# One level of Strassen's scheme in both feed-forward products of a float32 kernel for retention and a squared-ReLU feed-forward

## The chip, the cores and the metric

The kernel runs on one core of a Trainium2 chip. Its time is the device time of one execution in microseconds. The kernel before was run three times; the time before is the median of these.

## What is computed

```python
# q, k, v: (8, 8, 576, 64) float32; w_in (512, 2048), w_out (2048, 512) float64
scores = matmul(q, k.T) / sqrt(64)
Dmat   = where(t >= s, gamma[h] ** (t - s), 0)        # gamma = 1 - 2**(-5 - h)
x      = matmul(scores * Dmat, v)                      # retention, per batch and head
x      = x.transpose(0, 2, 1, 3).reshape(4608, 512)    # 8 * 576 tokens, d_model 512
out    = square(maximum(x @ w_in, 0)) @ w_out          # (4608, 512) float32
```

Both weights come in as float64, as their bits, and are rounded to float32 on the chip.

## The kernel before

Retention goes over 40 chunks of 128 tokens (the fifth of each batch of 576 has 64). For chunk i, `turn(i)` transposes q and k on TensorE (VectorE scales q by gamma^t, ScalarE copies k); `scores(i)` makes the masked scores `ret0` and `ret1`, one for each head of a pair, and `vs`, v scaled by gamma^-s; `retain(i)` makes the chunk's x, transposed, from `ret` and `vs` and from U, the sum of k^T v' over the chunks before it in its batch. U of a pair of heads lies on the diagonal of a 128 x 128 block `u_sb`. The main loop interleaves `retain(i-2)`, `scores(i-1)` and `turn(i)`, and after each of the three calls `ffn(tokens / 3)`.

The feed-forward part works on nine blocks of 512 tokens. Block n starts when its x, `xT[n]`, is complete. `ffn_in(n, m)` makes one of 16 tiles of 128 of d_ff: four matmuls of 512 columns into PSUM, ReLU on ScalarE into `r`, the square on VectorE into `g`. `ffn_out(n, ts, part)` sums a quarter of d_ff for 128 tokens; after the last quarter VectorE copies the sum and POOL's queue stores it. `ffn` takes such steps from a list at a rate set by the tokens. Both weights stay on chip for the whole run.

A weight piece (512 KB of float64 bits) is fetched by `fetch_w` and rounded by `round_w`: five passes on VectorE (L122, L127 to L130) with two on POOL (L123, L125) between the first and the fourth. `prepare` rounds the next piece and fetches two ahead: three pieces for each turn of the main loop at the start, then one for each feed-forward step.

Order: every engine takes its instructions in the order in which the code issues them, and waits on semaphores. A tile pool gives out `bufs` buffers in turn; who writes to one waits until the last user of it has finished. DMAs of inputs and weights are issued on SP's queue, in that order, and a wait there holds back what follows.

Of the kernel before, what the change touches and what calls it, by code (L numbers as in the profile page):

```python
# [10 lines left out]
U32 = mybir.dt.uint32  # L11
AF = mybir.ActivationFunctionType
# [4 lines left out]
N_LD = 4  # chunks of q, k and v on chip at once  # L17
# [3 lines left out]
def kernel(  # L21
# [23 lines left out]
    nc = tc.nc  # L45
# [3 lines left out]
    HP = H // 2  # pairs of heads: a pair fills the 128 partitions  # L49
# [4 lines left out]
    N_DF = d_ff // 128  # L54
    N_BLK = n_tok // TOK
# [17 lines left out]
    ps_f = ctx.enter_context(tc.tile_pool(name="ps_f", bufs=2, space=PS))  # L73
# [23 lines left out]
    raws = []

    def fetch_w(j):
        t, src = w_tile(j)  # L100
        w.append(t)
        if src.dtype == F32:
            nc.sync.dma_start(t, src)
            raws.append(None)
            return
        raw = raw_pool.tile([128, N_DM, 128], src.dtype, tag="raw", name="raw")
        nc.sync.dma_start(raw, src)
        raws.append(raw)

    def round_w(j):  # L110
        """float64 bits to the nearest float32: (mantissa) * 2^(exponent), and the sign.
# [3 lines left out]
        if raws[j] is None:  # L115
            return
# [239 lines left out]
```

## Time and profile before

| | us |
|---|---|
| median of 3 runs | 1265.71 (1264.05 to 1266.25) |
| span of the profiled execution | 1263.9 |
| TensorE busy | 1222.0 |
| VectorE busy | 313.0 |
| ScalarE busy | 154.4 |
| GpSimd (POOL) busy | 74.9 |

The profiled execution's own time is not given apart from the runs; its span is the time from its first to its last instruction. PE is TensorE's matmul side, PEld its weight loads, DVE VectorE, ACT ScalarE, SPq and POOLq the queues that issue DMAs. L numbers are lines of the kernel. In the trace a float32 matmul of the code is two MATMUL instructions, each with a weight load of its own, and a transpose is one.

### The profile page before, as it was taken

How to read it: one execution, taken by the hardware profiler on the slowest of the kernel's cores; microseconds unless marked ns; L12 is line 12 of the kernel's file. 1: busy time of each engine (PE TensorE's matmuls, PEld its weight loads, DVE VectorE, ACT ScalarE, POOL GpSimd, SP SyncE). 2: the span in 40 equal slices, each digit the busy share in tenths (PEclk: the TensorE clock that was granted, in tenths of full speed). 3: DMA queues.
4: the chain of work that ended last, by engine and by line, in shares of the span. 5: the costliest groups of instructions: out<-in, count | busy, mean ns of one | idle time of the engine just before them, and what ended most of it. 6: DMA issues, size and time to landing. Idle time of an engine off the chain costs nothing.

```text
span 1263.9 us, 10515 instructions
## 1 busy us (share of the span) xinstructions
PE 1222.0 (97%) x4416; PEld 609.8 (48%) x4416; DVE 313.0 (25%) x500; ACT 154.4 (12%) x293; POOL 74.9 (6%) x110
## 2 busy tenths in 40 slices
PE   3698999999999999999999999999999999999998
PEld 2454544544445554445544554454544544444443
DVE  4888811221122112221112112211221122101200
ACT  1111100210012001110121001100210012000100
POOL 2333300000000000000000000000000000000000
PEclk9698999999999999999999999999999999999999
DMA  9655412001210112001110111101121000000000
GB/s 237 180 142 154 117 42 59 5 17 42 59 30 17 33 30 46 21 25 34 42 34 13 34 42 26 42 21 33 25 50 30 26 9 1 9 17 8 1 9 25
DMA packets 126479, 56.41 MB, mean 45 GB/s; under 512 B 113760, under 2 KB 121952, under 8 KB 126304
## 3 DMA queue, kind: packets, MB, share of 16 engines
q1 hardware_dynamic: 123552, 46.30, 15.9%
q0 software_dynamic: 2880, 9.44, 1.9%
q8 instruction: 35, 0.57, 0.2%
q14 instruction: 12, 0.10, 0.0%
HBM read 46.29 MB, written 9.44 MB: 44 GB/s over the span
## 4 chain that ended last, share of the span: by engine, by line
issue 72%; PE 18%; POOL 4%; DVE 4%; SPq 1%; DMA 0%; POOLq 0%
PE o_ps L262 8%; PE h_ps L248 7%; POOL exp L125 1%; POOL out_dram L268 1%; SPq L82 1%; POOL exp L123 1%; PE x_ps L215 1%; DVE w_in L129 1%; DVE w_in L130 1%; PE x_ps L212 1%; PE sc L193 1%; PE u_ps L231 1%; DVE exp L122 1%; DMA raw<-in_moe_w_in_dram 0%; DVE ret L198 0%
## 5 line engine op out<-in xcount | busy, mean ns | idle before, releaser
L248 PE MATMUL h_ps<-xT,w_in 128*128 128x512 f32 x1152 | 509.4, 596 | 0.0
L262 PE MATMUL o_ps<-w_out,g 128*128 128x512 f32 x1152 | 506.7, 594 | 0.0
L248 PEld LDWEIGHTS h_ps<-xT,w_in 128*128 128x128 f32 x1152 | 215.3, 191 | 253.0 <-issue 250.5
L262 PEld LDWEIGHTS o_ps<-w_out,g 128*128 128x128 f32 x1152 | 214.8, 190 | 253.5 <-issue 249.7
L253 DVE TENSOR_TENSOR g<-r 128x512 f32<-128x512 f32 x144 | 99.5, 691 | 405.6 <-ACT r L251 405.6
L251 ACT ACTIVATE r<-h_ps 128x512 f32<-128x512 f32 x144 | 86.0, 597 | 512.4 <-PE h_ps L248 487.5
L198 DVE TENSOR_TENSOR ret<-sc,msk 128x512 f32<-128x512 f32 (+1 forms) x80 | 47.0, 629 | 213.8 <-PE sc L193 213.8
L268 POOL DMA_DIRECT2D out_dram<-o_sb x36 | 19.6, 545 | 1084.0 <-DVE o_sb L266 1084.0
L266 DVE COPY o_sb<-o_ps 128x512 f32<-128x512 f32 x36 | 24.9, 692 | 202.1 <-PE o_ps L262 202.1
L215 PE MATMUL x_ps<-ret,vs 128*64 128x128 f32 (+1 forms) x640 | 65.0, 296 | 0.2 <-DVE vs L202 0.2
L212 PE MATMUL x_ps<-qT,u_sb 128*128 128x128 f32 (+1 forms) x256 | 60.3, 319 | 0.2 <-DVE ret L198 0.2
L212 PEld LDWEIGHTS x_ps<-qT,u_sb 128*128 128x128 f32 x256 | 42.4, 197 | 29.4 <-issue 27.8
L183 ACT COPY kT<-kT_ps 128x512 f32<-128x512 f32 (+1 forms) x40 | 21.7, 543 | 282.7 <-PE kT_ps L178 282.4
L193 PEld LDWEIGHTS sc<-qT,kT 64*128 64x128 f32 (+1 forms) x640 | 37.1, 183 | 32.1 <-issue 30.9
L225 ACT COPY xT<-x_ps 128x512 f32<-128x512 f32 (+1 forms) x44 | 22.0, 509 | 235.2 <-PE x_ps L215 235.2
L178 PE MATMUL kT_ps<-ident,k_ld 128*128 128x128 f32 (+1 forms) x160 | 25.1, 283 | 26.5 <-DVE ret L198 26.4
L181 DVE TENSOR_TENSOR qT<-qT_ps,dq 128x512 f32<-128x512 f32 (+1 forms) x40 | 25.3, 633 | 100.5 <-PE qT_ps L178 90.5
L193 PE MATMUL sc<-qT,kT 64*128 64x128 f32 (+1 forms) x640 | 44.5, 280 | 5.2 <-DVE qT L181 5.2
L215 PEld LDWEIGHTS x_ps<-ret,vs 128*64 128x64 f32 (+1 forms) x640 | 33.8, 141 | 20.7 <-issue 6.9
L231 PE MATMUL u_ps<-vs,k_ld 128*128 128x128 f32 x256 | 39.2, 299 | 0.0
L231 PEld LDWEIGHTS u_ps<-vs,k_ld 128*128 128x128 f32 x256 | 33.0, 201 | 6.0 <-issue 6.0
L178 PEld LDWEIGHTS kT_ps<-ident,k_ld 128*128 128x128 f32 (+1 forms) x160 | 18.8, 149 | 28.2 <-DVE ret L198 27.7
(25 smaller groups left out, 253.3 us busy)
## 6 DMA issues: line engine op xcount, KB each, us to landing
out_dram<-o_sb POOLq DMA_DIRECT2D x36, 256.0 KB, 2.3
q_ld<-in_q_dram SPq DMA_DIRECT2D x32, 256.0 KB, 4.5
k_ld<-in_k_dram SPq DMA_DIRECT2D x32, 256.0 KB, 3.3
v_ld<-in_v_dram SPq DMA_DIRECT2D x32, 256.0 KB, 4.1
raw<-in_moe_w_in_dram SPq DMA_DIRECT2D x16, 512.0 KB, 4.4
raw<-in_moe_w_out_dram SPq DMA_DIRECT2D x16, 512.0 KB, 3.4
dq<-in_decay_q_dram SPq DMA_DIRECT2D x1, 1152.0 KB, 7.1
q_ld<-in_q_dram SPq DMA_DIRECT2D x8, 128.0 KB, 2.9
```

What stands on the lines that cost most here:

```text
L178: nc.tensor.transpose(p[:, hp, :cs], loaded[i][j][:cs, 2 * hp:2 * hp + 2, :], ident[:cs, :cs])
L181: nc.vector.tensor_tensor(t[:, :, :cs], p[:, :, :cs], dq[:, :, c0:c0 + cs], op=ALU.mult)
L193: nc.tensor.matmul(sc[e][:cs, hp, :cs], lhsT=kT[sl, hp, :cs], rhs=qT[sl, hp, :cs], start=True, stop=True)
L198: nc.vector.tensor_tensor(r[:cs, :, :cs], sc[e][:cs, :, :cs], msk[:cs, :, :cs].to_broadcast([cs, HP, cs]), op=ALU.mult)
L212: nc.tensor.matmul(p[:, hp, :cs], lhsT=u_sb[ci % 2][:, hp, :], rhs=s["qT"][:, hp, :cs], start=True, stop=False, skip_group_check=True)
L215: nc.tensor.matmul(p[D * e:D * e + D, hp, :cs], lhsT=s["vs"][:cs, 2 * hp + e, :], rhs=s["ret"][e][:cs, hp, :cs], start=(ci == 0), stop=Tru ...
L231: nc.tensor.matmul(u_ps[0][:, hp, :], lhsT=loaded[i][1][:cs, 2 * hp:2 * hp + 2, :], rhs=s["vs"][:cs, 2 * hp:2 * hp + 2, :], start=(ci == 0 ...
L248: nc.tensor.matmul(p, lhsT=w[m][:, cc, :], rhs=xT[n][:, cc, :], start=(cc == 0), stop=(cc == N_DM - 1))
L251: nc.scalar.activation(r, p, AF.Relu)
L253: nc.vector.tensor_tensor(g[n, m], r, r, op=ALU.mult)
L262: nc.tensor.matmul(acc[0], lhsT=g[n, m][:, ts * 128:(ts + 1) * 128], rhs=w[N_DF + m].rearrange("p c f -> p (c f)"), start=(m == 0), stop=( ...
L268: nc.gpsimd.dma_start(out[row:row + 128, :], o)
```

## The change

The first block is still computed plainly, but its second product runs with d_ff outside: `first_out(m)` adds two tiles of d_ff to four sums in PSUM. Beside it POOL makes Strassen's sums of the weights: those of w_in in place and in `ws` (`sum_w_in`), those of w_out in a `stage` tile that then goes, with all seven operands, to DRAM (`w2_dram`). There are two `stage` tiles, and a pair of pieces of w_out is rounded straight into one.

From block 1 on both products are taken as 2 x 2 blocks in seven half-size products (`PRODUCTS`; each right operand is 256 columns wide). `sum_x` makes the sums of x, partly in place. `ffn_in(n, mp, j)` does product j for two pairs of d_ff tiles, and adds what comes out of PSUM to earlier parts on VectorE and ScalarE; POOL makes the sums of the squared values for the second product. `ffn_out(n, j, tt)` takes its right operand from `w2`, 1 MB for each product, which `fetch_w2` brings from DRAM for step j+2 when step j is done.

In retention, U and its part of x are made in tiles of 64 columns (of the lhsT), so that only the diagonal of U is computed; `vs` moves from VectorE to POOL; `kT`, `ret` and `vs` have one buffer instead of two, q and v three instead of four. Fetched float64 bits and exponents lie in parts of `G` (g2 and g3) that are not yet in use. `ps_f` has four PSUM buffers of one kind instead of two of each of two kinds.

```diff
+PRODUCTS = (
+    ("A11", "B11", "a"), ("S2", "T2", "b"), ("S1", "T1", "c"), ("A12", "B21", "a"),
+    ("S3", "T3", "b"), ("S4", "B22", "c"), ("A22", "T4", "b"),
+)
+OPENS = {0, 1, 2}
+CLOSES = {3, 5, 6}
...
-    ps_f = ctx.enter_context(tc.tile_pool(name="ps_f", bufs=2, space=PS))
+    ps_f = ctx.enter_context(tc.tile_pool(name="ps_f", bufs=4, space=PS))
+    wa = [const.tile([128, N_DM, 128], F32, name=f"wa{m}") for m in range(N_M)]
+    wb = [const.tile([128, N_DM, 128], F32, name=f"wb{m}") for m in range(N_M)]
+    ws = [const.tile([128, 3, 2, 128], F32, name=f"ws{m}") for m in range(N_M)]
+    G = [const.tile([128, 7, 2, HT], F32, name=f"g{j}") for j in range(N_M // 2)]
+    w2_dram = dram.tile([7, 128, N_M, d_model // 2], F32, name="w2_dram")
...
+    def piece_dst(j):
+        wi, m, e = pieces[j]
+        if wi == 0:
+            return (wb if e else wa)[m].rearrange("p c f -> p (c f)")
+        if e == 0:
+            stage[m] = w2_pool.tile([128, N_M, d_model // 2], F32, tag="w2", name="w2_stage")
+        return stage[m][:, 2 * e:2 * e + 2, :].rearrange("p a b -> p (a b)")
...
     def retain(i):
...
             if ci > 0:
-                nc.tensor.matmul(p[:, hp, :cs], lhsT=u_sb[ci % 2][:, hp, :], rhs=s["qT"][:, hp, :cs], ...)
+                for e in range(2):
+                    half = slice(D * e, D * e + D)
+                    nc.tensor.matmul(p[half, hp, :cs], lhsT=u_sb[ci % 2][:, hp, half], rhs=s["qT"][:, hp, :cs], ...)
...
-                nc.tensor.matmul(u_ps[0][:, hp, :], lhsT=loaded[i][1][:cs, 2 * hp:2 * hp + 2, :],
-                                 rhs=s["vs"][:cs, 2 * hp:2 * hp + 2, :], ...)
+                for e in range(2):
+                    nc.tensor.matmul(u_ps[0][D * e:D * e + D, hp, :], lhsT=loaded[i][1][:cs, 2 * hp + e, :],
+                                     rhs=s["vs"][:cs, 2 * hp + e, :], ...)
...
+    def first_in(m):                       # m: 0 to 15, tiles m // 2 and m // 2 + 8 in turn
...
+        r = work2.tile([128, TOK], F32, tag="qT", name="r")
+        nc.scalar.activation(r, p, AF.Relu)
+        nc.vector.tensor_tensor(g0(m + e * N_M), r, r, op=ALU.mult)
+    def sum_w_in(m):
+        nc.gpsimd.tensor_tensor(s1, a21, a22, op=ALU.add)
+        nc.gpsimd.tensor_tensor(s2, s1, a11, op=ALU.subtract)
+        nc.gpsimd.tensor_tensor(s4, a12, s2, op=ALU.subtract)
+        nc.gpsimd.tensor_tensor(a21, a11, a21, op=ALU.subtract)
+    def first_out(m):
+        s = stage[m]
+        for e in range(2):
+            for ts in range(N_TS):
+                nc.tensor.matmul(acc[ts], lhsT=g0(m + e * N_M)[:, ts * 128:(ts + 1) * 128],
+                                 rhs=s[:, 2 * e:2 * e + 2, :].rearrange("p a b -> p (a b)"), ...)
+        sum_w_in(m)
+        b11, b12, b21, b22, t1, t2, t4 = (s[:, j, :] for j in range(7))
+        nc.gpsimd.tensor_tensor(t1, b12, b11, op=ALU.subtract)
+        nc.gpsimd.tensor_tensor(t2, b22, t1, op=ALU.subtract)
+        nc.gpsimd.tensor_tensor(t4, b21, t2, op=ALU.subtract)
+        nc.gpsimd.tensor_tensor(b12, b22, b12, op=ALU.subtract)
+        nc.sync.dma_start(w2_dram[:, :, m, :].rearrange("o p d -> p o d"), s[:, 0:7, :])
...
+    def sum_x(n):
+        nc.vector.tensor_tensor(t1, b12, b11, op=ALU.subtract)
+        nc.vector.tensor_tensor(t2, b22, t1, op=ALU.subtract)
+        nc.gpsimd.tensor_tensor(b12, b22, b12, op=ALU.subtract)
+        nc.gpsimd.tensor_tensor(t4, b21, t2, op=ALU.subtract)
...
+    def ffn_in(n, mp, j):
+        if mp == 0 and j == 0:
+            for nxt in range(2):
+                fetch_w2(nxt)
+        left, right, to = PRODUCTS[j]
+        if j in OPENS:
+            sums[to] = ps_f.tile([128, 2, HT], F32, tag="f", name=f"h_{to}")
+        p = sums[to]
+        for mm in range(2):
+            w = w1(left, 2 * mp + mm)
+            for c in range(2):
+                nc.tensor.matmul(p[:, mm, :], lhsT=w[:, c, :], rhs=xs[n][right][:, c, :], ...)
+        def square(t):
+            nc.vector.scalar_tensor_tensor(t, t, 0.0, t, op0=ALU.max, op1=ALU.mult)
+        if j == 0:
+            nc.scalar.copy(p1, p)
+        elif j == 1:
+            nc.vector.tensor_tensor(u2, p, p1, op=ALU.add)
+        elif j == 2:
+            nc.scalar.copy(p15, p)
+            nc.vector.tensor_tensor(p15, p15, p1, op=ALU.add)
+        elif j == 3:
+            nc.scalar.activation(g["A11"], p, AF.Relu)
+            nc.gpsimd.tensor_tensor(g["A11"], g["A11"], g["A11"], op=ALU.mult)
+        elif j == 4:
+            nc.vector.tensor_tensor(g["A22"], p, p15, op=ALU.add)
+            square(g["A22"])
+        elif j == 5:
+            nc.vector.tensor_tensor(g["S1"], p, u2, op=ALU.add)
+            square(g["S1"])
+            nc.gpsimd.tensor_tensor(g["S3"], g["A11"], g["S1"], op=ALU.subtract)
+            nc.gpsimd.tensor_tensor(g["S1"], g["S1"], g["A22"], op=ALU.add)
+            nc.gpsimd.tensor_tensor(g["S2"], g["S1"], g["A11"], op=ALU.subtract)
+        else:
+            nc.vector.tensor_tensor(g["A12"], p, p1, op=ALU.add)
+            square(g["A12"])
+            nc.gpsimd.tensor_tensor(g["S4"], g["A12"], g["S2"], op=ALU.subtract)
+    def ffn_out(n, j, tt):
...
+        for m in range(N_M):
+            nc.tensor.matmul(p[:, tt, :], lhsT=G[m // 2][:, G_SLOT[left], m % 2, tt * 128:(tt + 1) * 128],
+                             rhs=w2[j][:, m, :], ...)
+        if tt == 0:
+            return
+        if j + 2 < len(PRODUCTS):
+            fetch_w2(j + 2)
...
+    def block_steps(n):
+        if n == 0:
+            return ([(4, first_in, m) for m in range(N_DF)] + [(8, first_out, m) for m in range(N_M)])
+        return ([(2, ffn_in, n, mp, j) for mp in range(N_M // 2) for j in range(len(PRODUCTS))]
+                + [(4, ffn_out, n, j, tt) for j in range(len(PRODUCTS)) for tt in range(2)])
     def ffn(tokens):
-        owed[0] += tokens * PER_TOK
-        while steps and owed[0] >= 1:
+        owed[0] += tokens * 118 / TOK
+        while steps and owed[0] >= steps[0][0]:
+            cost, f, *args = steps.pop(0)
+            for _ in range(cost // 4 if f in (first_in, first_out) else 0):
+                prepare(min(len(pieces) - 1, 2 * N_M + 3 + (2 * args[0] if f == first_out else 0)))
```

How the instructions stand on the engines, at three places. First TensorE, around the end of the `retain` of chunk 11 (the second of the third batch), with block 1's second product on either side of it. Before (`o_ps` is a sum of the second product, `g` its left operand; a row is one matmul of the code, or several alike):

```order
L212 MATMUL x_ps_1594<-qT_1466,u_sb0_132 128x128
L215 MATMUL x_ps_1594<-ret0_1542,vs_1546 64x128
L215 MATMUL x_ps_1594<-ret1_1544,vs_1546 64x128
L231 MATMUL u_ps_1387<-vs_1546,k_ld_1212 128x128 x4
L262 MATMUL o_ps_1589<-w_out4_636,g_1289 128x512
L262 MATMUL o_ps_1589<-w_out5_677,g_1318 128x512
L262 MATMUL o_ps_1589<-w_out6_713,g_1343 128x512
L262 MATMUL o_ps_1589<-w_out7_747,g_1366 128x512
```

Now (`o_a` and `o_b` are sums of two of Strassen's products, `w2` their right operands, g0 to g3 the tiles of `G`):

```order
L258 MATMUL x_ps_1618<-qT_1449,u_sb1_148 64x128 x2
L262 MATMUL x_ps_1618<-ret0_1542,vs_1546 64x128
L262 MATMUL x_ps_1618<-ret1_1544,vs_1546 64x128
L279 MATMUL u_ps_1487<-vs_1546,k_ld_1160 64x64 x8
L431 MATMUL o_a_1609<-w2_1286,g0_116 128x256 x2
L431 MATMUL o_a_1609<-w2_1286,g1_117 128x256 x2
L431 MATMUL o_a_1609<-w2_1286,g2_118 128x256 x2
L431 MATMUL o_a_1609<-w2_1286,g3_119 128x256 x2
L431 MATMUL o_b_1659<-w2_1288,g0_116 128x256 x2
```

Columns of 512 became 256, U's parts became 64 wide and twice as many.

Second VectorE in block 0, where pieces of w_out are rounded; before, while the first product runs (`w_out4` and `w_out5` are pieces that stay on chip):

```order
L122 TENSOR_SCALAR exp_716<-raw_637 128x512 [waits DMAHW6_49]
L127 TENSOR_SCALAR w_out4_636<-raw_637 128x512
L128 SCALAR_TENSOR_TENSOR w_out4_636<-raw_637,w_out4_636 128x512 [waits DVE_49]
L129 SCALAR_TENSOR_TENSOR w_out4_636<-w_out4_636,exp_716 128x512 [waits DVE_49,Pool_49]
L130 SCALAR_TENSOR_TENSOR w_out4_636<-raw_637,w_out4_636 128x512 [waits DVE_49]
L253 TENSOR_TENSOR g_731<-r_729 128x512 [waits Activation_49]
L181 TENSOR_TENSOR qT_738<-qT_ps_733,dq_96 128x512 [waits PE_49]
```

Now, behind the scores that follow `first_out(0)` (`w2_stage_925` is the third `stage` tile, in the first one's buffer; its second write waits for a DMA and for POOL):

```order
L240 TENSOR_TENSOR ret1_920<-sc1_909,msk_144 128x512 [waits PE_49]
L165 TENSOR_SCALAR g3_119<-g2_118 128x512 [waits DMAHW6_49]
L170 TENSOR_SCALAR w2_stage_925<-g2_118 128x512 [waits DMAHW6_49,Pool_49]
L171 SCALAR_TENSOR_TENSOR w2_stage_925<-g2_118,w2_stage_925 128x512 [waits DVE_49]
L172 SCALAR_TENSOR_TENSOR w2_stage_925<-w2_stage_925,g3_119 128x512 [waits DVE_49,Pool_49]
L173 SCALAR_TENSOR_TENSOR w2_stage_925<-g2_118,w2_stage_925 128x512 [waits DVE_49]
L165 TENSOR_SCALAR g3_119<-g2_118 128x512 [waits DMAHW7_49]
L170 TENSOR_SCALAR w2_stage_925<-g2_118 128x512
```

The rounding of w_out moved from the first product, a piece a step, to the second, two pieces a step, into buffers that are used again.

Third POOL at the same place. Before, only exponents (two passes a piece) stand there:

```order
L123 TENSOR_SCALAR exp_943<-exp_943 128x512 [waits DVE_49]
L125 TENSOR_SCALAR exp_943<-exp_943 128x512 [waits Pool_49]
L123 TENSOR_SCALAR exp_963<-exp_963 128x512 [waits DVE_49]
L125 TENSOR_SCALAR exp_963<-exp_963 128x512 [waits Pool_49]
L123 TENSOR_SCALAR exp_980<-exp_980 128x512 [waits DVE_49]
```

Now (the exponents of the pair for the third `stage` tile, in g3, then the sums of `first_out(1)`; the last waits for TensorE, and SP's store of that tile waits for it):

```order
L166 TENSOR_SCALAR g3_119<-g3_119 128x512 [waits DVE_49]
L168 TENSOR_SCALAR g3_119<-g3_119 128x512 [waits Pool_49]
L166 TENSOR_SCALAR g3_119<-g3_119 128x512 [waits DVE_49]
L168 TENSOR_SCALAR g3_119<-g3_119 128x512 [waits Pool_49]
L307 TENSOR_TENSOR ws1_109<-wb1_101 128x256
L308 TENSOR_TENSOR ws1_109<-ws1_109,wa1_93 128x256 [waits Pool_49]
L309 TENSOR_TENSOR ws1_109<-wa1_93,ws1_109 128x256 [waits Pool_49]
L310 TENSOR_TENSOR wb1_101<-wa1_93,wb1_101 128x256
L328 TENSOR_TENSOR w2_stage_654<-w2_stage_654 128x256
L329 TENSOR_TENSOR w2_stage_654<-w2_stage_654 128x256 [waits Pool_49]
L330 TENSOR_TENSOR w2_stage_654<-w2_stage_654 128x256 [waits Pool_49]
L331 TENSOR_TENSOR w2_stage_654<-w2_stage_654 128x256 [waits PE_49]
```

Eight two-input passes for each `first_out` were added behind the exponents of a later pair.

More of the change, by code (lines that the diff above doesn't have):

```diff
@@ L96 @@
-    w = []
-    raws = []
-    def fetch_w(j):
[L100 to L104, printed above, removed]
-            return
[L106 to L116, printed above, removed]
-        words = raws[j].rearrange("p c f -> p (c f)").bitcast(U32).rearrange("p (n two) -> p n two", two=2)
+    pieces = [(wi, m, e) for wi in range(2) for m in range(N_M) for e in range(2)]
@@ L169 @@
     xT = {}
+    xs = {}
     u_ps = [None]
@@ new lines, in store @@
+    def store(n, half, o):
+        row = n * TOK + half * HT
+        nc.gpsimd.dma_start(out[row:row + HT, :].rearrange("(a p) d -> p a d", p=128), o)
+    def sum_x(n):
+        x = xT[n]
+        b11, b12 = x[:, 0:2, 0:HT], x[:, 0:2, HT:]
+        b21, b22 = x[:, 2:4, 0:HT], x[:, 2:4, HT:]
+        t = work.tile([128, 3, 2, HT], F32, tag="xs", name="xs")
+        t1, t2, t4 = (t[:, j, :, :] for j in range(3))
+        nc.vector.tensor_tensor(t1, b12, b11, op=ALU.subtract)
+        nc.vector.tensor_tensor(t2, b22, t1, op=ALU.subtract)
+        nc.gpsimd.tensor_tensor(b12, b22, b12, op=ALU.subtract)
+        nc.gpsimd.tensor_tensor(t4, b21, t2, op=ALU.subtract)
+        xs[n] = {"B11": b11, "T3": b12, "B21": b21, "B22": b22, "T1": t1, "T2": t2, "T4": t4}
```

204 lines of the change are left out of this document (134 added, 70 removed).

## The prediction

> **What bounds the kernel now.** I read the busy times by engine first, then who waited for whom on TensorE, then TensorE's timeline.
>
> ```profile
> span 1263.9 us, 10515 instructions
> PE 1222.0 (97%) x4416; PEld 609.8 (48%) x4416; DVE 313.0 (25%) x500; ACT 154.4 (12%) x293; POOL 74.9 (6%) x110
> ...
> PE   3698999999999999999999999999999999999998
> ...
> PE kT_ps L178 <- DVE ret L198: 26.4, 5, 6.9
> ```
>
> The third row is TensorE's busy share, in tenths, in 40 slices of 31.6 us; the last is from the list of waits (us in total, times, longest). TensorE is the only full engine. Most of its 42 us of idle time lies in the first slices, where VectorE rounds weights and hands `ret` over late. So the time follows the number and length of TensorE's instructions, wherever nothing else stops it. A float32 matmul of the code is two MATMULs in the trace; a transpose is one.
>
> ```profile
> 1148.25 55.10 PE L248 MATMUL h_ps<-xT,w_in 128*128 128x512 f32 x128
> 1203.18 55.10 PE L262 MATMUL o_ps<-w_out,g 128*128 128x512 f32 x128
> ```
>
> The last block runs bare: 128 instructions between the two starts, (1203.18 - 1148.25)/128 = 0.4291 us per 512-column instruction. A block of 256 of them costs 109.9 us, nine blocks 989 of the 1263.9 us.
>
> **Both products by Strassen, blocks 1 to 8.** Seven half-size products replace eight: 7 x 16 matmuls in each product, 448 instructions of 256 columns per block. No such instruction exists before; the nearest rows are these: TensorE's timeline (start us, length us), then weight loads by line (busy us, mean ns).
>
> ```profile
> 673.16 0.60 PE L178 MATMUL qT_ps<-ident,q_ld 128*128 128x128 f32 x4
> 673.60 0.60 PE L178 MATMUL kT_ps<-ident,k_ld 128*128 128x128 f32 x4
> 674.04 7.03 PE L248 MATMUL h_ps<-xT,w_in 128*128 128x512 f32 x16
> ...
> L178 PEld LDWEIGHTS kT_ps<-ident,k_ld 128*128 128x128 f32 x128 | 16.2, 152 | 25.4 <-DVE ret L198 25.0 <-DMA k_ld<-in_k_dram 0.4
> L248 PEld LDWEIGHTS h_ps<-xT,w_in 128*128 128x128 f32 x1152 | 215.3, 191 | 253.0 <-issue 250.5
> ```
>
> Four 128-column transposes start in 0.44 us, 0.110 each. A line through 0.110 at 128 and 0.4291 at 512 columns gives 0.2164 at 256. A load of 191 ns still fits beside that. Block: 448 x 0.2164 = 96.9; gain 12.9, times 8: **-103 us**. Bounds: half a 512-column instruction (0.2146) gives -110; the 128-column matmuls of `u_ps` (below, 8 in 1.00 us, 0.125 each, change of array tiling included) put the line at 0.226 and the gain at -68. I take the transposes' line, whose loads are as wide and which carry no change of tiling.
>
> Here a rule of the Trainium skill speaks against the change. "TensorE: Matmul & The Clock Gate", in Part 3, under what overlaps and what doesn't, says that weight loads overlap running matmuls only when their row groups differ; all these are full-height. By it an instruction would cost load plus matmul, 0.191 + 0.214 = 0.405 us, a block 181 us, the whole some 570 us more instead of 103 less. The trace does not bear it out: transposes with loads of 152 ns start every 110 ns, all rows in use. The rule in full is the far end of rival (4).
>
> **Retention in 64-column tiles.** TensorE's timeline in the middle of the span: a chunk that reads U, a 64-row chunk's scores, a batch's first chunk.
>
> ```profile
> 651.14 0.38 PE L212 MATMUL x_ps<-qT,u_sb 128*128 128x128 f32 x2
> 651.46 0.44 PE L215 MATMUL x_ps<-ret,vs 128*64 128x128 f32 x4
> ...
> 654.19 1.16 PE L231 MATMUL u_ps<-vs,k_ld 128*128 128x128 f32 x8
> 655.19 7.03 PE L248 MATMUL h_ps<-xT,w_in 128*128 128x512 f32 x16
> 662.15 0.68 PE L193 MATMUL sc<-qT,kT 64*64 64x64 f32 x16
> 662.76 10.57 PE L248 MATMUL h_ps<-xT,w_in 128*128 128x512 f32 x24
> ...
> 702.84 1.09 PE L215 MATMUL x_ps<-ret,vs 128*64 128x128 f32 x16
> 703.86 1.16 PE L231 MATMUL u_ps<-vs,k_ld 128*128 128x128 f32 x8
> 704.86 7.03 PE L262 MATMUL o_ps<-w_out,g 128*128 128x512 f32 x16
> ```
>
> A chunk that reads U takes 3.05 us for x (changing tiling twice per pair) and 1.00 for U, 4.05. A first chunk's 16 x-instructions, all in 64-column tiles, take 1.02: 0.064 each. Afterwards x is 32 such instructions, 2.04, without a change of tiling. U becomes 16 instructions of 64 columns; the `sc` of a 64-row chunk, also 64 columns, takes 0.61 for 16, so 0.61 (bound: 1.02). The chunk falls by 1.40, a first chunk by 0.39; a batch's fifth chunk (64 rows, no U after it) stays. Without the five chunks of the start: 21 x 1.40 + 7 x 0.39 = **-32 us**. Bound: U's half-width instructions do not run side by side (0.110 each), -6.
>
> **The start.** Rounding keeps VectorE ahead of all else in the first two slices, where TensorE waits for it; five `vs` of 0.68 us move from it to POOL, which has room: **-3 us** (bounds 0 and -3.4). `kT`, `ret`, `vs` lose a buffer each, but their last readers stand ahead in TensorE's order: 0. In `first_in` ScalarE's `r` shares `qT`'s two buffers and can wait for a `retain`; the four buffers of `ps_f` let TensorE run on: 0. If that cover is gone, a step of 3.4 us is lost per chunk.
>
> **Block 0's second product, the term against.** Before, each piece of w_out was rounded into a place of its own, ahead of use. Now a pair is rounded into one of two `stage` tiles. `stage` m+2 needs the tile of m free: TensorE done with `first_out`(m), eight POOL passes, the store to DRAM landed. The orders above show the loop: VectorE's first write to `stage` 2 waits for that store; everything on VectorE queues behind, the second piece's exponent pass too; on POOL its two exponent passes stand ahead of the eight sums of m+1, and SP's next store waits for the last of those. So one round is wholly serial. The rows below are groups by line and shape (busy us, mean ns of one, then idle time before them), and DMA issues (KB each, us to landing).
>
> ```profile
> L123 POOL TENSOR_SCALAR exp<-exp 128x512 uint32<-128x512 uint32 x32 | 23.2, 725 | 97.5 <-DVE exp L122 97.5
> L125 POOL TENSOR_SCALAR exp<-exp 128x512 uint32<-128x512 uint32 x32 | 30.0, 937 | 2.6
> L122 DVE TENSOR_SCALAR exp<-raw 128x512 uint32<-128x512 uint32 x32 | 13.4, 419 | 5.4 <-DMA raw<-in_moe_w_in_dram 5.4
> L128 DVE SCALAR_TENSOR_TENSOR w_out<-raw,w_out 128x512 f32<-128x512 uint32 x16 | 15.7, 980 | 0.5
> L129 DVE SCALAR_TENSOR_TENSOR w_out<-w_out,exp 128x512 f32<-128x512 f32 x16 | 11.1, 692 | 8.2 <-POOL exp L125 8.2
> L130 DVE SCALAR_TENSOR_TENSOR w_out<-raw,w_out 128x512 uint32<-128x512 uint32 x16 | 11.1, 692 | 0.5
> L181 DVE TENSOR_TENSOR qT<-qT_ps,dq 128x256 f32<-128x256 f32 x8 | 3.4, 420 | 19.1 <-PE qT_ps L178 19.1
> L193 PE MATMUL sc<-qT,kT 64*128 64x128 f32 x512 | 39.0, 294 | 5.2 <-DVE qT L181 5.2
> L202 DVE TENSOR_TENSOR vs<-v_ld,dv 128x512 f32<-128x512 f32 x32 | 21.8, 681 | 0.0
> ...
> out_dram<-o_sb POOLq DMA_DIRECT2D x36, 256.0 KB, 2.3
> raw<-in_moe_w_in_dram SPq DMA_DIRECT2D x16, 512.0 KB, 4.4
> raw<-in_moe_w_out_dram SPq DMA_DIRECT2D x16, 512.0 KB, 3.4
> ```
>
> A round: first piece, 0.42 (a pass of the kind of L122) + 0.98 + 0.69 + 0.69 = 2.78; exponent of the second 0.42; POOL's two passes 0.73 + 0.94; handing over 0.1: 5.0. Eight POOL sums of 128x256 with two inputs: no row; VectorE's 128x256 pass (0.42) and twice POOL's dearest pass per element (0.94) bound it, I take the middle, 0.68: 5.4. The store, 896 KB in 1 KB pieces: 256 KB lands in 2.3, 512 KB in 3.4 to 4.4; the line gives 5.0 to 7.5, and 4.4 is least (384 KB more than 512 at 377 GB/s, a row below); I take 5.7, nearer the lower line, since w_in's median was taken in the crowded start. Together **16.1 us a round** (bounds 12.8 and 20.0), against 6.9 us of TensorE work in `first_out` and some 1.3 of retention.
>
> After `first_out`(0): 6.4 until its store has landed, five rounds (80.5), two pieces rounded (6.4), `first_out`(7) 6.9, one `vs` 1.2: 101. Unhindered, TensorE needs 7 x 6.87 = 48.1 plus two scores (39.0 us in 32 chunks, 1.2 each), two turns (0.88 each, from the transposes) and two retains (2.65 each), 57.6. **+44 us**, bounds +26 and +65.
>
> The Trainium skill's "GPSIMD Engine Reference", section 4.1, has two-input passes at about half VectorE's rate. By it a sum would take 0.84 us (twice the 0.42 row), a round 17.4, this term 51 us and the total 1184; no trace row here shows a two-input pass on POOL.
>
> **The rest.** Per pair of d_ff tiles (28 x 2 instructions, 12.1 us) VectorE gets eight passes of 0.69, 5.5 us, ScalarE three, POOL five (at 1.36 by the price above, 6.8 us). PSUM is read a step of 1.73 us ahead of its next use: 0. The sums of x (four passes) run beside the scores and the first step: 0. If the passes take longer, step 6, which adds to the tile that step 4 filled, is late first. The second product fetches 1 MB of w2 per step, two ahead; from the end of step j the fetch has step j+1, 32 x 0.2164 = 6.9 us.
>
> ```profile
> 134.00:135.00 1.00, 1.00 (x8) 0.71 (x7) 0.61 (x1) 0.38 (x1) 0.92 (x2) 1.00 0.95 377
> 708.00:709.00 1.00, 1.00 (x4) 0.44 (x3) 0.00 (x0) 0.00 (x0) 0.00 (x0) 1.00 1.16 236
> ```
>
> The last column is GB/s. 512 KB of w_out land in 3.4; another 512 KB at 377 GB/s take 1.4: 4.8, 0.5 for SP, 5.3 in all, 1.6 us to spare. A chunk's load ahead of it (768 KB of 256-byte pieces at 236 GB/s, 3.3 us) makes it some 1.7 late, about once a block: bounds 0 and 17, taken **+4 us**. SP's waits ahead of a fetch are for `vs` two steps before, done by then: 0. The tail stores 512 KB where 256 were stored: **+1 us**.
>
> Sum: 1263.9 - 103 - 32 - 3 + 44 + 4 + 1 = 1174.9. The profiled execution's own time is not listed; the median of the runs shown, 1265.71, is 1.8 above its span, and I add that difference: **1177 us**, own range 1150 to 1210.
>
> **Rivals.** (1) Block 0's rounds overlap (POOL or the store far faster than the rows say): 1177 - 44 = 1133. Against it stands the fixed order on POOL. (2) PSUM is read too late in the first product; 1 us per pair of tiles, 32 pairs: 1209. For it: eight passes more per pair on VectorE beside retention's. (3) The w2 fetches run at the rate of w_in's pieces (4.4 for 512 KB, 2.1 more than for 256): 1 MB in 8.6, 9.1 with the issue, 2.2 late, 40 fetches: 1177 + 88 - 4 = 1261. Against: w_out's 4 KB pieces land in 3.4. (4) Slower than before: weight loads do not fit beside 256-column matmuls. Apart from Strassen the terms add up to +14, so it decides from a gain under 14 us, 8 x (109.9 - 448 t) = 14, t = 0.241 us per instruction. At 0.26 the kernel takes 1265.7 + 14 + 53 = 1333. For it: loads of 191 ns would fill 88% of the time; against: the transposes.
>
> **How the numbers follow.** Forecast 0.67, rivals 0.12, 0.10, 0.06, 0.05 in order. 1135 to 1225 leaves out (3), (4) and about half of (1). A change under 0.2% (2.5 us) could not be told from none; only chance between (3) and (4) falls there, 0.01. Faster 0.94, slower 0.05.
>
> **What would show it.** 256-column instructions start every 0.216 us; TensorE waits for VectorE's `w_stage` line some 44 us between 140 and 245 us, and hardly after; retained chunks take 2.65 us; the waits for w2 stay under 17 us. I am wrong if the first spacing is above 0.23, if the wait in block 0 is under 26 or over 65, or if TensorE idles over 2% after block 0.

## The result, and the profile after

The changed kernel takes 1168.08 us (1167.34 to 1168.70), the kernel before 1265.98 in the same comparison: ratio 0.9226, 95% interval 0.9213 to 0.9239. The profiled span fell from 1263.9 to 1165.6 us. One execution below, of `exps_first`, ran at a granted clock of 0.66 and took 1611.57 us; it is in no comparison. The head of the page and TensorE's row of its slices (29.1 us each):

```profile
span 1165.6 us, 15121 instructions
PE 1081.1 (93%) x6464; PEld 881.0 (76%) x6464; DVE 416.7 (36%) x610; ACT 146.2 (13%) x287; POOL 387.3 (33%) x372
...
PE   3496987679999999999999999999999999999998
```

TensorE has 2048 more instructions and is 141 us less busy. The hollow in slices 6 to 9 (seen as 8, 7, 6, 7) is new: block 0's second product. Who waited for whom on TensorE:

```profile
PE kT_ps L220 <- DVE ret L240: 36.6, 5, 9.6
PE acc_ps L322 <- DVE w_stage L173: 30.1, 5, 7.4
PE sc L235 <- DVE qT L223: 6.3, 3, 4.6
```

The first row had 26.4 us before; the second is the prediction's wait for `w_stage`; no row has w2. The last block, TensorE's timeline, with the first step of each product and the last step:

```profile
1062.95 1.89 PE L381 MATMUL h_a<-xT,wa 128*128 128x256 f32 x8
...
1111.30 7.07 PE L431 MATMUL o_a<-w,g 128*128 128x256 f32 x32
...
1152.74 7.07 PE L431 MATMUL o_b<-w,g 128*128 128x256 f32 x32
```

224 instructions of the first product in 48.35 us and 192 of the second in 41.44: 0.2159 and 0.2158 us per 256-column instruction.

The ledger is cut where block 1's first step begins, in before and then after:

```profile
214.22 7.13 PE L248 MATMUL h_ps<-xT,w_in 128*128 128x512 f32 x16
```

```profile
251.10 1.99 PE L381 MATMUL h_a<-xT,wa 128*128 128x256 f32 x8
```

| stretch | before | after | difference | by the prediction's terms |
|---|---|---|---|---|
| up to block 1 | 214.2 | 251.1 | +36.9 | -3 + 44 - 4.6 (chunks 5 to 8) = +36.4 |
| from block 1 on | 1049.7 | 914.5 | -135.2 | -103 - 27.5 + 4 + 1 = -125.5 |

In the second stretch TensorE is 99.3% busy (busy us by engine, then granted clock, DMA share, GB/s):

```profile
251.10:1165.60 914.50, 907.91 (x5588) 786.14 (x5584) 280.46 (x405) 118.92 (x232) 279.74 (x232) 1.00 0.33 99
```

### The profile page after: what moved, and what is told of

It reads as the page before. It is cut to its first block, busy times and chain, and to the rows that moved or that the text cites. A ratio compares the mean times of both kernels' runs of the same rounds, so it can differ in the third digit from the quotient of the medians.

```text
span 1165.6 us, 15121 instructions
## 1 busy us (share of the span) xinstructions
PE 1081.1 (93%) x6464; PEld 881.0 (76%) x6464; DVE 416.7 (36%) x610; ACT 146.2 (13%) x287; POOL 387.3 (33%) x372
## 4 chain that ended last, share of the span: by engine, by line
PE 79%; POOL 7%; DVE 6%; issue 4%; DMA 3%; SPq 1%; POOLq 0%; DVEq 0%
PE h_b L381 14%; PE o_b L431 13%; PE h_c L381 9%; PE h_a L381 9%; PE o_a L431 9%; PE o_c L431 8%; PE h_ps L297 3%; PE sc L235 3%; PE x_ps L262 3%; PE x_ps L258 2%; DMA w_dram<-w_stage 2%; POOL g L168 2%; POOL g L166 2%; PE acc_ps L322 1%; PE kT_ps L220 1%
## 5 line engine op out<-in xcount | busy, mean ns | idle before, releaser
L431 PE MATMUL o_b<-w,g 128*128 128x256 f32 x768 | 172.5, 381 | 0.0
L431 PEld LDWEIGHTS o_b<-w,g 128*128 128x128 f32 x768 | 144.5, 190 | 19.9
L381 PE MATMUL h_a<-xT,wa 128*128 128x256 f32 x512 | 122.5, 382 | 0.0
L431 PE MATMUL o_c<-w,g 128*128 128x256 f32 x512 | 115.4, 381 | 0.0
L431 PE MATMUL o_a<-w,g 128*128 128x256 f32 x512 | 114.9, 381 | 0.0
L431 PEld LDWEIGHTS o_c<-w,g 128*128 128x128 f32 x512 | 96.2, 190 | 13.6
L431 PEld LDWEIGHTS o_a<-w,g 128*128 128x128 f32 x512 | 96.3, 190 | 13.3
L381 PEld LDWEIGHTS h_a<-xT,wa 128*128 128x128 f32 x512 | 95.8, 190 | 13.7
L322 PE MATMUL acc_ps<-w_stage,g 128*128 128x512 f32 x128 | 67.6, 688 | 30.1 <-DVE w_stage L173 30.1
L408 POOL TENSOR_TENSOR g<-g 128x512 f32<-128x512 f32 x32 | 40.6, 1269 | 118.7 <-DVE g L389 115.4
L389 DVE SCALAR_TENSOR_TENSOR g<-g 128x512 f32<-128x512 f32 x96 | 75.4, 786 | 3.3
L244 POOL TENSOR_TENSOR vs<-v_ld,dv 128x512 f32<-128x512 f32 (+1 forms) x40 | 42.2, 1055 | 98.8 <-issue 80.6
L400 POOL TENSOR_TENSOR g<-g 128x512 f32<-128x512 f32 x32 | 33.2, 1037 | 119.1 <-ACT g L399 114.7
```

The lines of the kernel that those rows point to most:

```text
L244: nc.gpsimd.tensor_tensor(vs[:cs], loaded[i][2][:cs], dv[:cs, :, ci:ci + 1].to_broadcast([cs, H, D]), op=ALU.mult)
L322: nc.tensor.matmul(acc[ts], lhsT=g0(m + e * N_M)[:, ts * 128:(ts + 1) * 128], rhs=s[:, 2 * e:2 * e + 2, :].rearrange("p a b -> p (a b)"), ...
L381: nc.tensor.matmul(p[:, mm, :], lhsT=w[:, c, :], rhs=xs[n][right][:, c, :], start=(j in OPENS and mm == 0 and c == 0), stop=(j in CLOSES a ...
L389: nc.vector.scalar_tensor_tensor(t, t, 0.0, t, op0=ALU.max, op1=ALU.mult)
L400: nc.gpsimd.tensor_tensor(g["A11"], g["A11"], g["A11"], op=ALU.mult)
L408: nc.gpsimd.tensor_tensor(g["S3"], g["A11"], g["S1"], op=ALU.subtract)
```

## The experiments

**1. Retention in 128-column tiles again (`wide_u`).** All else as in the changed kernel.

```diff
-                for e in range(2):
-                    half = slice(D * e, D * e + D)
-                    nc.tensor.matmul(p[half, hp, :cs], lhsT=u_sb[ci % 2][:, hp, half], rhs=s["qT"][:, hp, :cs],
-                                     start=(hp == 0), stop=False, skip_group_check=True)
+                nc.tensor.matmul(p[:, hp, :cs], lhsT=u_sb[ci % 2][:, hp, :], rhs=s["qT"][:, hp, :cs],
+                                 start=True, stop=False, skip_group_check=True)
...
-                for e in range(2):
-                    nc.tensor.matmul(u_ps[0][D * e:D * e + D, hp, :], lhsT=loaded[i][1][:cs, 2 * hp + e, :],
+                nc.tensor.matmul(u_ps[0][:, hp, :], lhsT=loaded[i][1][:cs, 2 * hp:2 * hp + 2, :],
...
```

> The changed kernel with retention's U and its part of x in 128-column tiles again, as before. Theory from the two timelines: a chunk that reads U costs 4.05 us of TensorE instead of 2.36, a batch's first chunk 2.02 instead of 1.49, a fifth 2.40 instead of 2.11; outside the start that is 21 x 1.69 + 7 x 0.53 + 7 x 0.29 = 41 us, so 1209 us. Rival, the prediction's term: 32 us, so 1200. Second rival, the column tiles were not worth anything on the path: 1168.

1201.55 us (1200.53 to 1202.25), ratio to the kernel before 0.9496 (0.9482 to 0.9511): 33.5 us slower than the changed kernel. One chunk that reads U, TensorE's timeline, first of the changed kernel, then of this one:

```profile
313.62 0.44 PE L258 MATMUL x_ps<-qT,u_sb 128*64 128x128 f32 x4
...
315.42 0.64 PE L279 MATMUL u_ps<-vs,k_ld 128*64 128x64 f32 x16
315.98 3.72 PE L431 MATMUL o_a<-w,g 128*128 128x256 f32 x16
```

```profile
317.70 0.38 PE L256 MATMUL x_ps<-qT,u_sb 128*128 128x128 f32 x2
...
320.75 1.16 PE L275 MATMUL u_ps<-vs,k_ld 128*128 128x128 f32 x8
321.74 2.54 PE L427 MATMUL o_a<-w,g 128*128 128x256 f32 x11
```

2.36 against 4.04 us; a first chunk takes 1.49 against 2.02, a fifth 2.11 against 2.40. After block 0 that is 18 x 1.68 + 6 x 0.53 + 7 x 0.29 = 35.5 us; the stretch from block 1 on is 30.8 us shorter (945.3 against 914.5). The 4.7 us between the two lie at the seams, where TensorE goes over to the narrow tiles and back. Around a chunk that reads U, a step of eight instructions takes 1.82 us ahead of it and 1.83 behind it, against 1.73 on both sides with wide tiles; a first or fifth chunk has one such seam more than with wide tiles: 18 x 0.19 + 13 x 0.1 = 4.7. Ahead of block 1 the narrow chunks take some 15 us less (3.4, 3.0 and 3.4 in the first three that read U), but only 4.0 us of the time is saved, since VectorE sets the pace there (8).

**2. The 64-column tiles alone, in the kernel before (`tiles_only`).** The same lines of the retention in the new form.

```diff
-                nc.tensor.matmul(p[:, hp, :cs], lhsT=u_sb[ci % 2][:, hp, :], rhs=s["qT"][:, hp, :cs],
-                                 start=True, stop=False, skip_group_check=True)
+                for e in range(2):
+                    half = slice(D * e, D * e + D)
+                    nc.tensor.matmul(p[half, hp, :cs], lhsT=u_sb[ci % 2][:, hp, half], rhs=s["qT"][:, hp, :cs],
+                                     start=(hp == 0), stop=False, skip_group_check=True)
...
```

> The kernel before with only the retention's 64-column tiles. The prediction's term: 1266 - 32 = 1234 us. Theory from the changed kernel with wide tiles again (1201.5 us, 33.5 us slower) and its rows (a chunk with U 4.04 -> 2.36 us, some 0.2 us of it given back at the seams, nothing gained before VectorE's rounding ends at 105 us): 1266 - 34 = 1232 us, x and U of a chunk in 2.36 us here too. Rival: the full saving of the rows, 1.69 us per chunk with U, 0.54 per first chunk and 0.29 per fifth, in all chunks but the first five: 1266 - 41 = 1225 us.

1229.68 us (1228.40 to 1230.96), ratio 0.9715 (0.9699 to 0.9731): -36.2 us, nearer the theory's 34 than the 41 of the bare rows. A chunk that reads U takes 2.36 us here too, with the same seams: 41 less 21 x 0.19 + 14 x 0.1 = 5.4 us is 35.6. So the two halves of the change add, within some 3 us.

**3. w_in's sums moved into the first product (`sums_early`).** The four POOL sums of w_in leave block 0's rounds, so a round keeps only w_out's four.

```diff
         nc.vector.tensor_tensor(g0(m + e * N_M), r, r, op=ALU.mult)
+        if e == 1:
+            sum_w_in(m)
...
-        sum_w_in(m)
```

> The changed kernel with the four sums of w_in moved out of first_out: POOL makes them in the first product, right behind the second tile of each pair. Theory (a round of block 0's second product is one serial chain, rounding, exponent, eight POOL sums, store): each of five rounds loses 0.72 + 1.06 + 1.06 + 0.90 = 3.7 us, from 16.7 to 12.9, so 1168 - 19 = 1149 us. Rival, the store or the rounding alone sets the round: no change, 1168. Second rival, POOL's sums beside VectorE's rounding delay the first product by as much: 1160 or more.

1155.78 us (1154.28 to 1158.14), ratio 0.9137 (0.9122 to 0.9152): -12.3. TensorE's waits:

```profile
PE kT_ps L220 <- DVE ret L240: 37.7, 5, 13.1
PE acc_ps L324 <- DVE w_stage L173: 15.5, 7, 4.4
```

The second product gave most of the theory's 19 us: from its first `first_out` to block 1 it takes 90.7 us (150.91 to 241.61) instead of 106.4, and the wait halves. But it begins at 150.91 instead of 144.73: the wait at `turn`(6) in the first product grew from 9.6 to 13.1 us. (Another 2.1 us are there from the start: the first product begins at 68.16 instead of 66.04, and in the other kernels alike up to there between 66.2 and 67.9.) The sums were not free where they went.

**4. Both exponent passes of a pair ahead of its first write to `stage` (`exps_first`).** So POOL has the second piece's exponents before VectorE blocks on the store.

```diff
+    def exp_w(j):
...
-        nc.vector.tensor_scalar(exp, hi, 20, 0x7FF, op0=ALU.logical_shift_right, op1=ALU.bitwise_and)
-        nc.gpsimd.tensor_scalar(exp, exp, 1151.0, 896.0, op0=ALU.min, op1=ALU.max)
-        nc.gpsimd.tensor_scalar(exp, exp, -896.0, 2.0 ** 23, op0=ALU.add, op1=ALU.mult)
+        exp_w(j)
+        if j >= 2 * N_M and j % 2 == 0:
+            exp_w(j + 1)
```

> The changed kernel with the exponent passes of both pieces of a pair issued ahead of the first write to the stage tile; nothing is added or left out. Theory (POOL's eight sums stand behind an exponent pass that waits for the last store, which makes two buffers work as one): the sums then run while the store of the tile before is under way, two rounds overlap, a pair of rounds takes 2 x 2.6 rounding + 2.9 POOL + 5 store = 13 us against 16.4 of TensorE work, and nearly all of the 42 us in block 0 go: 1130 us (to 1136). Rival, the round is long because of the work in it and not of its order: at most 2 us gained, 1166.

1149.10 us (1148.59 to 1149.11), ratio 0.9081 (0.9066 to 0.9096): -19.0, half of what the theory had. The rounds are read from the next kernel, which has the same time.

**5. The same with `r` in buffers of its own (`exps_r`).** `r` of the first product goes into `o`'s two tiles, unused until block 0 ends.

```diff
-        r = work2.tile([128, TOK], F32, tag="qT", name="r")
+        r = o_pool.tile([128, 2, d_model], F32, tag=f"o{e}", name="r")[:, 0, :]
```

> Both exponent passes of a pair ahead of its first write to stage, and r in o's buffers. Theory: the two edits act in different stretches and add: 1168.1 - 19.0 (the exponents moved alone) - 3.7 = 1145.4 us; the store still landing, then TensorE's first_out waits for two full pieces rounded one after the other beside POOL's sums: VectorE's four passes on a piece take 3.5 to 4.2 us instead of 2.8. Rival: the earlier start is given back as waiting in block 0's second product, where VectorE is full: then 1149 us.

1149.15 us (1148.16 to 1149.48), ratio 0.9075 (0.9061 to 0.9088): the rival's figure. One piece of a pair on VectorE and the sums on POOL at the same time, two timelines:

```profile
196.42 0.82 DVE L180 TENSOR_SCALAR w_stage<-g 128x512 uint32<-128x512 uint32 x1 [3.52 <-DMA w_dram<-w_stage]
197.28 1.10 DVE L181 SCALAR_TENSOR_TENSOR w_stage<-g,w_stage 128x512 f32<-128x512 uint32 x1
198.47 1.03 DVE L182 SCALAR_TENSOR_TENSOR w_stage<-w_stage,g 128x512 f32<-128x512 f32 x1
199.53 1.10 DVE L183 SCALAR_TENSOR_TENSOR w_stage<-g,w_stage 128x512 uint32<-128x512 uint32 x1
```

```profile
195.43 0.72 POOL L317 TENSOR_TENSOR ws<-wb 128x256 f32<-128x256 f32 x1
...
198.92 1.17 POOL L338 TENSOR_TENSOR w_stage<-w_stage 128x256 f32<-128x256 f32 x1
...
202.04 1.17 POOL L341 TENSOR_TENSOR w_stage<-w_stage 128x256 f32<-128x256 f32 x1
```

The rounding now runs beside the sums, which is what the edit wanted, and both get longer: a piece takes 4.1 us on VectorE (196.42 to 200.56, the next piece's start) instead of 2.6, eight sums 7.8 (195.43 to 203.21) instead of 5.8 at 0.72 each. A round falls from 16.65 to 11.8 and 12.9 us (VectorE's first writes to `stage` at 196.42, 208.22 and 221.07), not to TensorE's 7 to 9. Two rounds are still one chain, 24.5 us from one pair's first sum to that of the pair after next (195.43 to 219.90): sums 7.8, store 5.0, rounding of a pair 8.1, the rest, mostly exponents, 3.6. The theory's 13 us had left out the sums, which the store has to wait for, and had nothing for the lengthening, 2.0 us on the sums and 2.9 on the pair. That is where the other half went.

**6. One-input passes on POOL (`one_input`).** The sums of weights, x and g are left out; each becomes a copy of one operand, at the same place.

```diff
-        nc.gpsimd.tensor_tensor(s1, a21, a22, op=ALU.add)
+        nc.gpsimd.tensor_scalar(s1, a21, 1.0, 0.0, op0=ALU.mult, op1=ALU.add)
...
```

> Every two-input POOL pass outside vs becomes a one-input pass of the same shape (it copies one operand), so sums of weights, x and g are left out; order, stores and all else as in the changed kernel. Theory: VectorE's passes that read both operands from SBUF lengthen (0.69 to 0.95 us in block 0, 0.79 us for the squares of blocks 1 to 8) only while POOL runs two-input passes; here they return to 0.69 us, POOL's eight sums fall from 6.8 us to 3.3 (half the 128x512 passes of 0.73 and 0.94 us), a round from 16.65 to about 12.6 us, the time by five rounds to 1148 us; nothing changes from block 1 on. Rival: VectorE is slowed by DMA traffic or by POOL working at all: the passes stay at 0.78 to 0.95 us, the round at 13.1 us and the time at 1150 us or above.

1151.68 us (1151.21 to 1152.03), ratio 0.9096 (0.9082 to 0.9109): -16.4 instead of -20; the round is 13.86 us. VectorE's groups (busy us, mean ns, idle before), first of the changed kernel, then of this one:

```profile
L389 DVE SCALAR_TENSOR_TENSOR g<-g 128x512 f32<-128x512 f32 x96 | 75.4, 786 | 3.3
L397 DVE TENSOR_TENSOR g<-g 128x512 f32<-128x512 f32 x32 | 24.2, 758 | 60.6 <-ACT g L396 60.6
L412 DVE TENSOR_TENSOR g<-h_b,g 128x512 f32<-128x512 f32 x32 | 22.1, 692 | 19.3 <-PE h_b L381 19.3
L172 DVE SCALAR_TENSOR_TENSOR w_stage<-w_stage,g 128x512 f32<-128x512 f32 x16 | 15.0, 937 | 6.1 <-POOL g L168 5.6
```

```profile
L389 DVE SCALAR_TENSOR_TENSOR g<-g 128x512 f32<-128x512 f32 x96 | 70.4, 733 | 3.3
L397 DVE TENSOR_TENSOR g<-g 128x512 f32<-128x512 f32 x32 | 22.1, 692 | 60.6 <-ACT g L396 60.6
L172 DVE SCALAR_TENSOR_TENSOR w_stage<-w_stage,g 128x512 f32<-128x512 f32 x16 | 13.0, 812 | 6.2 <-POOL g L168 5.6
```

Neither story fits whole. The lengthening shrinks with POOL's time but does not vanish, so one-input passes cause it too. VectorE's passes that take one operand from PSUM, as L412, stay at 692 ns in the changed kernel, though all 32 run beside a POOL pass. Those that lengthen here have both operands in SBUF, while POOL reads SBUF.

**7. `r` in buffers of its own, alone and with both moves (`after_r`, `both_r`).** The edit of 5, in the changed kernel and in the kernel of 9.

> The changed kernel with r of the first product in o's two buffers, which are free until block 0 ends, instead of qT's two. Theory: sharing qT's buffers is what lengthened TensorE's wait in the first product (turn(6)'s kT_ps, 9.6 us against 5.9 us in the kernel before), because r waits for a retain and VectorE's queue stands behind the squaring of r. Then that wait falls to about 6 us and the time by 3.7 us, to 1164.4 us. Rival: the wait is VectorE's backlog of weight rounding, whatever r's buffer; then the wait stays near 9.6 us and the time at 1168 us.

> Sums of w_in in the first product, exponents of a pair ahead of its first write to stage, and r in o's buffers. Theory: in the first product TensorE waits 14.5 us at turn(6) because r's sharing holds VectorE's queue up; without it the wait falls to about the 5.9 us of the kernel before: 1142.05 - 8.6 = 1133.5 us. Rival: that wait comes from VectorE's squaring and rounding being stretched beside POOL's two-input sums, whatever r's buffer: the wait stays over 11 us and the time at 1139 us or above.

`after_r`: 1168.57 us (1167.40 to 1170.35), ratio 0.9231 (0.9217 to 0.9244). `both_r`: 1141.20 us (1140.04 to 1145.53), ratio 0.9025 (0.9005 to 0.9044). No change in either. The wait at `kT_ps` stays, in `after_r`:

```profile
PE kT_ps L220 <- DVE ret L240: 33.8, 5, 9.2
```

The theory that the shared buffers lengthened it is refuted; the sharing costs nothing, as the prediction had it.

**8. `vs` back on VectorE (`vs_back`).**

```diff
-        nc.gpsimd.tensor_tensor(vs[:cs], loaded[i][2][:cs],
+        nc.vector.tensor_tensor(vs[:cs], loaded[i][2][:cs],
```

> The changed kernel with vs on VectorE again, as in the kernel before. The prediction's term (five vs of 0.68 us taken off the full VectorE of the start): 3 us slower, 1171 us, the first product beginning after 68 us. Theory: each vs on POOL lengthens one of VectorE's two-input passes beside it from 0.69 to about 1.5 us, so the move gave nothing, and the earlier start came from the narrow tiles: 1166 to 1169 us, the passes w_in,exp of the first weights back at 0.69 us (now 0.90 to 1.01), the first product beginning near 66 us.

1168.50 us (1168.10 to 1169.41), ratio 0.9230 (0.9216 to 0.9243): no change. One VectorE group of the changed kernel, then of this one, and the first product's first step here:

```profile
L172 DVE SCALAR_TENSOR_TENSOR wa<-wa,g 128x512 f32<-128x512 f32 x8 | 8.1, 1009 | 4.1 <-POOL g L168 4.1
```

```profile
L172 DVE SCALAR_TENSOR_TENSOR wa<-wa,g 128x512 f32<-128x512 f32 x8 | 5.5, 692 | 4.1 <-POOL g L168 4.1
...
64.76 3.70 PE L297 MATMUL h_ps<-xT,wa 128*128 128x512 f32 x8
```

With `vs` on POOL, a VectorE pass beside it loses what VectorE had gained. The product begins no later without the move (64.76 against 66.04; 68.75 in before). The early start goes with the narrow tiles: `tiles_only`, with `vs` on VectorE, begins at 65.74, `wide_u`, with `vs` on POOL, at 69.78. And it is used up at once, because `turn`(6) waits for VectorE's rounding, in before and then after:

```profile
104.08 1.12 PE L178 MATMUL kT_ps<-ident,k_ld 128*128 128x128 f32 x4 [5.92 <-DVE ret L198]
```

```profile
105.21 1.11 PE L220 MATMUL kT_ps<-ident,k_ld 128*128 128x128 f32 x4 [9.63 <-DVE ret L240]
```

**9. Both moves, and a later place for the sums (`both`, `both_late`).** `both` has the edits of 3 and 4. `both_late` puts each pair's w_in sums behind the 8th and later steps of the first product, when VectorE's backlog is gone:

```diff
+    LATE = {7: 0, 8: 1, 9: 2, 10: 3, 11: 4, 12: 5, 14: 6, 15: 7}
...
-        if e == 1:
-            sum_w_in(m)
+        k = 2 * m + e
+        if k in LATE:
+            sum_w_in(LATE[k])
```

> The two edits together: exponents of a pair first, and w_in's sums in the first product. Theory: once the order is mended the sums are hidden and their place does not matter, 1130 us as with the exponents alone, within 4 us. Rival, the two savings add up: 19 us under the kernel with the exponents first alone.

> As the kernel with both moves (1142.05 us), but w_in's eight sums stand behind the 8th and later steps of the first product, when VectorE's rounding of the first weights is over. Theory: the sums early in the first product stretched VectorE's passes and so TensorE's wait at turn(6), 14.5 us against 9.6; here it returns to about 9.6 us and the time falls by 5 us, to 1137 us. Rival: the wait moves to block 0's second product, since POOL has less done when it begins: 1142 us or more.

`both`: 1142.05 us (1140.88 to 1142.37), ratio 0.9024 (0.9009 to 0.9039). `both_late`: 1138.73 us (1137.76 to 1140.21), ratio 0.8995 (0.8981 to 0.9008), the fastest here. The wait at `turn`(6) in `both`, then in `both_late`:

```profile
PE kT_ps L230 <- DVE ret L250: 39.2, 5, 14.5
PE acc_ps L334 <- DVE w_stage L183: 9.7, 5, 3.7
```

```profile
PE kT_ps L230 <- DVE ret L250: 39.4, 5, 11.5
PE acc_ps L337 <- DVE w_stage L183: 8.3, 4, 2.8
```

The longest wait fell by 3.0 us and the time by 3.3, direction and most of the size as expected; the rest of the wait above 9.6 was not traced further. The moves of 3 and 4 alone gave 12.3 and 19.0; together they give 26.0. That both spend the same VectorE and POOL time would explain it; this was not shown apart.

## Why the prediction was right, and where its steps were not

The time came 9 us under the forecast, inside its own range. The ledger puts the 9 us behind block 0: no wait for w2 (4), and somewhat more from retention (3) and Strassen (2) than forecast.

- **Strassen, blocks 1 to 8 (-103): right.** 448 x 0.2159 = 96.7 us a block against 109.9, -105.3 in all. Weight loads of 190 ns do hide beside 256-column instructions: PEld is busy 786 of 914 us and TensorE does not wait for it. The Trainium skill's "TensorE: Matmul & The Clock Gate", Part 3 (what overlaps and what doesn't), says that weight loads overlap matmuls only when their row groups differ. The prediction's estimate by it was 0.405 us per instruction; these runs contradict it for full-height loads.
- **Retention (-32): the size was right by luck, with errors that cancel.** `wide_u` gives 33.5, `tiles_only` 36.2. A chunk fell by 1.68 us, not 1.40: 16 of the 64-column x-instructions take 0.90 us (half of 1.80), 0.056 each instead of 0.064, and U's sixteen 0.56 us. A fifth chunk, which was to stay, fell by 0.29. Against that stand the seams, and chunks 7 and 8 in block 0's second product: their rows give 3.4 us, but that product is only 1.2 us shorter than in `wide_u` (147.54 to 255.07 there).
- **Start (-3): the step failed.** Moving `vs` was worth nothing (`vs_back`). The term took VectorE's passes off at their length but left out what the same passes on POOL do to VectorE. The earlier start went with the narrow tiles and was gone by 105 us.
- **`r` sharing `qT`'s buffers (0): right** (`after_r`).
- **Block 0's second product (+44): the size was right, the make-up not.** From the end of `first_out`(0), at 151.69, to 250.49 it took 98.8 us, against the prediction's 101 and 57.0 unhindered (57.6 with retains of 2.36): +42. But the wait at `w_stage` is 30.1 us, not 44; the other 11.5 are `first_out` running longer. Its five late steps take 8.6 to 10.1 us instead of 6.97:

```profile
174.82 9.90 PE L322 MATMUL acc_ps<-w_stage,g 128*128 128x512 f32 x16 [4.79 <-DVE w_stage L173]
...
208.11 8.62 PE L322 MATMUL acc_ps<-w_stage,g 128*128 128x512 f32 x16 [6.54 <-DVE w_stage L173]
...
241.63 8.92 PE L322 MATMUL acc_ps<-w_stage,g 128*128 128x512 f32 x16 [5.68 <-DVE w_stage L173]
```

```profile
170.00:241.60 71.60, 41.56 (x138) 19.12 (x136) 32.52 (x48) 2.46 (x8) 38.49 (x49) 0.79 0.48 136
```

The granted clock there is 0.79 (the third last column); from block 1 on it is 1.00. The chain's other links moved too. The first store goes out at 149.16, before `first_out`(0) has ended, so the first write to `stage` 2 comes 2.7 us after that end (154.42), where the chain had 6.4. Five rounds take 84.5 us instead of 80.5 (154.42 to 238.90). `first_out`(7) starts once the first piece of its pair is rounded, 2.7 us later instead of 6.4, takes 8.9 instead of 6.9, and no `vs` (1.2) follows: 2.7 + 84.5 + 2.7 + 8.9 = 98.8. The round of 16.1 us came out at 16.65 (from 174.82 to 208.11 are two): the sums 6.8 instead of 5.4, the store 5.0 instead of 5.7, the rounding and exponents some 4.8 instead of 5.0.

```profile
176.90 0.72 POOL L307 TENSOR_TENSOR ws<-wb 128x256 f32<-128x256 f32 x1
177.69 1.05 POOL L308 TENSOR_TENSOR ws<-ws,wa 128x256 f32<-128x256 f32 x1
...
182.99 0.72 POOL L331 TENSOR_TENSOR w_stage<-w_stage 128x256 f32<-128x256 f32 x1
```

By the Trainium skill's "GPSIMD Engine Reference", section 4.1, with two-input passes at about half VectorE's rate, the prediction had estimated 0.84 us per sum. An undisturbed one takes 0.72, the mean of all eight is 0.85 with VectorE in the way; the prediction's middle of 0.68 was too low.

- **The fetch of w2 (+4): nothing, the bound's lower end.** The DMA issues:

```profile
w<-w_dram SPq DMA_DIRECT2D x56, 1024.0 KB, 5.0
...
w_dram<-w_stage SPq DMA_DIRECT2D x8, 896.0 KB, 4.9
```

It lands in 5.0 us (4.8 was estimated). The prediction put a chunk's load directly ahead of a fetch. In the trace the load goes out behind the fetch of one step and 7 us ahead of the next (335.21 and 342.62), which is enough.

- **The tail (+1): 0.2.** From TensorE's end to the span's, 5.95 us against 5.78.
- **Rivals.** (2), PSUM read too late, did not come: 6.6 us idle in 914.5. (3) and (4) fell with the absent wait for w2 and the spacing of 0.216. (1) describes what the moves of 4 and 9 reach for: even `both_late` keeps 8.3 us of the wait.

## What to carry to other kernels

When work moves from VectorE to POOL, or new POOL work is laid beside VectorE, price the pair: of a VectorE pass with two SBUF operands and a POOL pass beside it, the one that begins second is held up, so the move can be worth nothing. A saving on TensorE counts only where TensorE sets the pace; ahead of a point that another engine reaches at a fixed time it becomes waiting. In a serial round, an overlap of two of its parts is worth the shorter part only if the two don't share a resource.

## What the runs showed of the hardware

VectorE and POOL get in each other's way, in numbers: a VectorE pass of 128x512 with both operands in SBUF takes 0.69 us alone, 1.03 to 1.21 beside POOL's 128x256 sums, and up to 1.54 beside the 128x512 `vs`; the sums go from 0.72 to 1.05 to 1.17. One-operand passes suffer too (0.42 to 0.94). It was already in the kernel before, where it looked like a property of the line: L128's 0.98 us, taken beside POOL's exponent passes, is 0.69 where POOL is idle (L171 of the changed kernel, a timeline row):

```profile
172.55 0.69 DVE L171 SCALAR_TENSOR_TENSOR w_stage<-g,w_stage 128x512 f32<-128x512 uint32 x1
```

So a duration read from a row contains the company it kept.

The pass that begins first keeps its length or nearly so, and the other waits for it. In the changed kernel, 82 VectorE passes of L171 to L173, L389 and L397 begin while a POOL pass runs, and 81 of them end 0.54 to 0.56 us after it, whether it is an exponent pass, a sum or `vs`. An example: `vs` runs from 17.37 to 18.42, the pass begun at 17.44 ends at 18.98. So a pass is lengthened by what is left of POOL's, less some 0.14 us. The other way round, a VectorE pass in `exps_r` ends at 198.38, and the sum begun within it, at 197.78, ends at 198.95, 0.57 us later.

The Trainium skill's "SBUF — State Buffer", in its section "Who interferes with whom", names the cause: the second SBUF operand of a VectorE instruction comes through a read port that POOL shares, so it contends with a POOL instruction that reads SBUF. The runs agree with who is affected, L412 with its PSUM operand included. It calls the shared pair of ports an exclusive lock, and the ends above fit that.

The granted clock is lower where TensorE waits a few us in every round: 0.70 to 0.82 in the five late steps of `first_out`. In `both_late`, with waits of 1.6 to 2.8 us there, it is 0.97 from 165 us to block 1. So a wait seems to cost more than its own length. No run here took that clock apart from the waits.
